# Reordering the first stages of an attention-plus-feed-forward kernel and splitting its last tile

## The chip, the cores and the metric

The kernel runs on one core of a Trainium2 chip. The core has five engines with instruction queues of their own, each worked off in order: TensorE (PE in the profile; its weight loads are listed as PEld), VectorE (DVE), ScalarE (ACT), GpSimd (POOL) and SyncE (SP). PE multiplies 128x128 blocks and writes to PSUM, a memory that the kernel divides into eight banks of 512 float32 values in each of 128 partitions; DVE and ACT read PSUM and write SBUF, the working memory. SP, ACT and POOL issue DMA transfers, which share 16 DMA engines.

The metric is device time in microseconds (us), the median of several executions. Beside it there is one profiled execution, whose span runs from its first to its last instruction.

## What is computed

Attention with a relative position bias over 8 batches and 8 heads of 576 positions, and then a bilinear feed-forward layer over the 4608 tokens:

```python
scores = scale * np.matmul(q, k.transpose(0, 1, 3, 2))      # q, k, v: 8 x 8 x 576 x 64
scores = scores + bias.transpose(2, 0, 1)[None, :, :, :]    # from a table of 32 buckets
scores = scores - np.max(scores, axis=-1, keepdims=True)
attn = np.exp(scores)
attn = attn / (np.sum(attn, axis=-1, keepdims=True) + 1e-09)
x = np.matmul(attn, v).transpose(0, 2, 1, 3).reshape(B * S, H * D)   # 4608 x 512
a = x @ w_a                                                 # 512 x 1536
b = x @ w_b
return (a * b @ w_out).astype(np.float32)                   # 1536 x 512
```

## The kernel before

**Units of work.** Heads are taken two at a time: 32 pairs, four to a batch. Of the 576 positions of a head, 512 are the main part (four tiles of 128) and 64 the tail; the tails of a pair's two heads share one tile. For pair `p`:

- `qk1(p, t)`: scores of key tile `t` against all main queries, one 512-column matmul per head, each on 64 rows of the array (in the profile the two start together). They go to one of two score buffers (`sc`, two banks each).
- `ex(p, t)`: ACT takes the exponential of both heads (128x1024) into an `at` tile, which frees the score buffer.
- `mul(p, t)`: DVE multiplies the part of `at` near the diagonal by the exponentials of the bias, `W`, which POOL and SP load from a small table in DRAM.
- `qk_tail`, `ex_tail`, `mul_tail`: the same for the tails (two exponentials on ACT).
- `av(p, j)`: query tile `j` of the product with v, with a column of ones that gives the sum; `norm(p, 0)` and `norm(p, 3)`: DVE's reciprocal and multiplication into `XG`, for tiles 0 to 2 and 3 to 4. Each frees an `av` bank.
- `t_x`, `c_x`: PE transposes `XG` and a copy puts it into `xn`, the feed-forward layer's input.
- `t_q`, `c_q`, `t_k`, `c_k` (pairs below 12): PE transposes q and k of a pair to come, and a copy puts them into `QT` and `KT`. For pairs 0, 1 and 3 this is done in float32 straight from `q32` and `k32` (`t32`, `q_next`, `k_next`; `tails_next` for the tails). From batch 3 on DMA does it.

The feed-forward layer is cut into nine chunks of 512 tokens. A chunk has 24 units, `ff_a` and `ff_b` for each of 12 blocks of 128 hidden columns (four matmuls; ACT copies `pa` to `ha`, DVE multiplies `pb` by `ha` into `g`), and 12 more, three parts for each of four output tiles (`ff_o`: four matmuls each; after the third ACT copies `po` to `ob` and SP stores it). The ninth chunk holds the tails of all heads, so each of its output tiles is stored in two DMAs (L536 to L538).

**Banks.** Two `sc` buffers (four banks), one bank `AV`, one `TR`, two of the pool `ffn` (`FF`). A bank of a pool is given to the next tile that asks for it once everything that reads it is done. From pair 12 on the feed-forward units also use `TR`.

**Order.** It is written out by hand (`manual_schedule`): each engine gets its instructions in the order in which the Python code makes them. First come the loads. SP and ACT issue those of pairs 0 and 1 in float32 (L184 to L187) and of the tails, POOL all others, one after another. PE starts with matmuls on a tile of zeros, `warm_up(5)` at L215 and L219, with the table's matmul between them. Then the transposes of pair 0 (L561 to L571), its first two score tiles (L572, L573), a loop over pairs 0 to 2 (L601 to L638), pair 3 and the start of pair 4 written out (L644 to L695), and from L714 a loop over pairs 4 to 32 that lays feed-forward units (`U`) between the steps of pair `s` and the `av` steps of pair `s - 1`. `quotas` says how many units a pair gets, and they are spread evenly over its `U` places. What is left of the units comes at L765.

Behind `k_next(0)` DVE sets one element of the tiles of pair 3 (L611, L612), and SP's loads of pair 3 (L613, L614) wait for that.

Of the kernel before, what the change touches and what calls it, by code (L numbers as in the profile page):

```python
# [13 lines left out]
def kernel(  # L14
# [11 lines left out]
    nc = tc.nc  # L26
    FP32 = mybir.dt.float32
# [9 lines left out]
    DM = 512  # L37
# [142 lines left out]
    def load32(p, src, out, engs):  # L180
        for h in range(2):
            load_h(engs[h], src, out[:, p, :, h, :], 0, 2 * p + h)
# [27 lines left out]
    def warm_up(n):  # L210
        for _ in range(n):
            nc.tensor.matmul(out=warm[:, :], lhsT=zero_sb[:, 0:128], rhs=zero_sb[:, :],
                             start=True, stop=True)
# [2 lines left out]
    tps = ps_av.tile([128, 512], FP32, tag="av", name="tab_ps")  # L216
    nc.tensor.matmul(out=tps[0:H, 0:NR], lhsT=bt_sb[0:NB, :], rhs=oh_sb[0:NB, :],
                     start=True, stop=True)
    warm_up(5)  # L219
    nc.scalar.activation(out=tab_sb[0:H, 127:127 + NR], in_=tps[0:H, 0:NR], func=ACTF.Exp)  # L220
    nc.scalar.dma_start(out=tab.ap(), in_=tab_sb[0:H, :])

# [108 lines left out]
        nc.sync.dma_start_transpose(  # L331
            out=dst[i][:, :, :, :].rearrange("d t h p -> d (t h) p"), in_=src[i][:, :])

    def qk1(p, t):
        qT = qT_(p)
        ps = ps_sc.tile([128, 2, 512], FP32, tag="sc", name=f"qk{p}_{t}")
        for hh in range(2):
            r = slice(64 * hh, 64 * hh + 64)
            nc.tensor.matmul(out=ps[:, hh, :], lhsT=kT_(p, t)[r, :],  # L339
                             rhs=qT[r, :, :], start=True, stop=True)  # L340
        st[p]["ps", t] = ps

    def qk(p, t0):
        qk1(p, t0)
        qk1(p, t0 + 1)

    def ex(p, t):
        ps = st[p]["ps", t]
        at = atp.tile([128, 2, SM], BF16, tag="at", name=f"at{p}_{t}")
        nc.scalar.activation(out=at[:, :, :], in_=ps[:, :, :], func=ACTF.Exp, scale=scale)  # L350
        st[p]["at", t] = at

    def mul(p, t):
        at, w = st[p]["at", t], W_sb[p % 4]
        lo, hi = max(0, 128 * (t - 1)), min(SM, 128 * (t + 2))
        y = 383 - (lo - 128 * (t - 1))
        z = y - (hi - lo)
        nc.vector.tensor_tensor(out=at[:, :, lo:hi], in0=at[:, :, lo:hi],  # L358
                                in1=w[:, :, y:(None if z < 0 else z):-1], op=MULT)
# [21 lines left out]
    def mul_tail(p):  # L381
        hp = p % 4
        at, w = att_sb[p % 2], W_sb[hp]
        nc.vector.tensor_tensor(out=at[:, 896:1088], in0=at[:, 896:1088],
                                in1=Wt_sb[:, hp, ::-1], op=MULT)
        x = at[:, 0:512].rearrange("p (h t c) -> p h t c", h=2, t=NM)[:, :, NM - 1, :]
        nc.vector.tensor_tensor(out=x, in0=x, in1=w[:, :, 127:63:-1], op=MULT)
# [86 lines left out]
    def c_x(p, eng=None):  # L474
        b, hp = divmod(p, 4)
        if p in XD:
            return
        ps = st[p]["x"]
        main, rest = xc(b)
        copy(eng, xn_sb[hp][:, main], ps[:, 0:SM])  # L480
        copy(eng, xn_sb[hp][:, rest], ps[:, SM:S])
# [36 lines left out]
    def ff_b(c, df, m0=0):  # L518
        ff_mm(c, df, wb_sb, "pb", m0, NMC)
        nc.vector.tensor_tensor(out=g_sb[df][:, :], in0=ff["pb"][:, :], in1=ff["ha"][:, :], op=MULT)  # L520

    def ff_o(c, tt, part):
        if part == 0:
            ff["po"] = ff_bank(f"po{c}_{tt}")
        po = ff["po"]
        for df in range(4 * part, 4 * part + 4):
            nc.tensor.matmul(out=po[:, :], lhsT=g_sb[df][:, 128 * tt:128 * tt + 128],  # L527
                             rhs=wo_sb[:, df, :], start=(df == 0), stop=(df == NDF - 1))
        if part == 2:
            ob = obp.tile([128, DM], FP32, tag="ob", name=f"ob{c}_{tt}")  # L530
            nc.scalar.activation(out=ob[:, :], in_=po[:, :], func=ACTF.Copy)  # L531
            if c < B:
                r0 = S * c + 128 * tt
                nc.sync.dma_start(out=out[r0:r0 + 128, :], in_=ob[:, :])
            else:
                for hh in range(2):  # L536
                    r0 = S * (2 * tt + hh) + SM
                    nc.sync.dma_start(out=out[r0:r0 + ST, :], in_=ob[64 * hh:64 * hh + 64, :])  # L538

    units = []  # L540
    for c in range(NCH):
        for df in range(NDF):
            m0 = 3 if c == 0 and df == 0 else 0
            units.append(lambda c=c, df=df, m0=m0: ff_a(c, df, m0))
            units.append(lambda c=c, df=df, m0=m0: ff_b(c, df, m0))
        for tt in range(4):
            for part in range(3):
                units.append(lambda c=c, tt=tt, part=part: ff_o(c, tt, part))
    nxt = 0

    def put_units(n):
# [18 lines left out]
    copy(None, QT[0][:, 256:512], psq1[:, 256:512])  # L570
    copy(None, KT[0][:, 128:SM], psk1[:, 128:512])  # L571
    qk1(0, 0)  # L572
    qk1(0, 1)  # L573

    def q_next(s):
        ps = bank(TR, BF16 if s == 1 else FP32, f"trq{s + 1}")
# [21 lines left out]
        for i in range(n):  # L598
            copy(eng, KT[(p0 + i) % 2][:, SM:SM + 256], ps[:, 256 * i:256 * i + 256])

    for s in range(3):  # L601
        ex(s, 0)
        if s > 0:
            mul(s - 1, 3)
            mul_tail(s - 1)
        q_next(s)
        qk1(s, 2)
        ex(s, 1)
        k_next(s)
        if s == 0:  # L610
            nc.vector.memset(q32[0:1, 3, 0, 0, 0:1], 0.0)  # L611
            nc.vector.memset(k32[0:1, 3, 0, 0, 0:1], 0.0)  # L612
            load32(3, q, q32, (nc.sync, nc.sync))  # L613
            load32(3, k, k32, (nc.sync, nc.sync))  # L614
        qk1(s, 3)
        ex(s, 2)
        if s == 0:
            tails_next(0, 2, None)
        else:
            tails_next(s + 1, 1, ACT)  # L620
        qk_tail(s)
        mul(s, 0)
        if s > 0:
            av(s - 1, 0)
            av(s - 1, 1)
            av(s - 1, 2)
            norm(s - 1, 0)
        mul(s, 1)
        ex(s, 3)
        if s > 0:  # L630
            av(s - 1, 3, FF)
        qk1(s + 1, 0)
        ex_tail(s)
        if s > 0:
            av(s - 1, 4)
            norm(s - 1, 3)
        mul(s, 2)
        qk1(s + 1, 1)  # L638

# [26 lines left out]
    t_x(2, FF)  # L666
    mul(3, 1)
    av_part(3, 0)
    c_x(2)
    t_q(4, FF)  # L670
    t_k(4, FF)
    c_q(4, ACT)
# [8 lines left out]
    qk1(4, 0)  # L681
    ex(4, 0)
    qk1(4, 1)
    ff_mm(0, 0, wa_sb, "pa", 0, 3)
    norm(3, 0)
    ex(4, 1)
    norm(3, 3)
    t_x(3, AV, range(3))
    ff_mm(0, 0, wb_sb, "pb", 0, 3)
    t_x(3, AV, range(3, 5))  # L690
    qk1(4, 2)
    ex(4, 2)
    c_x(3)
    qk1(4, 3)
    ex(4, 3)  # L695

    def tails4():
        ps = bank(TR, BF16, "trt4")
# [15 lines left out]
    for s in range(4, NP + 1):  # L714
        new = s < NP
        U = "unit"
        A = lambda *jq: (lambda: [av(s - 1, j, AV if j < 3 or s >= R3 else TR) for j in jq])
        N = lambda j: (lambda: norm(s - 1, j))
        steps = []
        if s == R3:  # L720
            ring3 = True
        if s == 4:
            steps += [U, tails4, lambda: mul(4, 0), U, lambda: qk_tail(4), lambda: ex_tail(4), lambda: mul(4, 1), U, lambda: mul(4, 2),
                      U, lambda: mul(4, 3), lambda: mul_tail(4), U, lambda: t_q(5, TR), lambda: c_q(5),
                      U, lambda: t_k(5, TR), lambda: c_k(5)]
        elif new:
            e = early((s + 1) // 4)
            steps += [lambda: qk(s, 0), lambda: ex(s, 0), U, lambda: ex(s, 1), A(0, 1, 2), N(0), U,
                      lambda: mul(s, 0), A(3, 4), N(3)]
            if s - 1 in XD:  # L730
                steps += [lambda: t_x(s - 1), lambda: turns(s)]
            steps += [U, lambda: mul(s, 1), lambda: qk(s, 2), lambda: ex(s, 2)]
            if e:
                steps += [lambda: t_q(s + 1, TR), lambda: c_q(s + 1)]
            steps += [U, lambda: ex(s, 3)]
            if e:
                steps += [lambda: t_k(s + 1, TR), lambda: c_k(s + 1)]
            steps += [U, lambda: mul(s, 2), U, lambda: mul(s, 3),
                      lambda: qk_tail(s), lambda: ex_tail(s), U]
            if s - 1 not in XD:  # L740
                steps += [lambda: t_x(s - 1, TR), lambda: c_x(s - 1), lambda: turns(s)]
            steps += [U, lambda: mul_tail(s), U]
        else:
            steps += [A(0, 1, 2), N(0), U, A(3, 4), N(3), U, lambda: t_x(s - 1, AV),
                      lambda: c_x(s - 1), U, U, U, U, U, U, U]
        quota = quotas.get(s, 9)
        seen, put = 0, 0
        nu = sum(1 for x in steps if x is U)
        for x in steps:
            if x is U:  # L750
                seen += 1
                n = (quota * seen + nu - 1) // nu - put
                put_units(n)
                put += n
            else:
                x()
        b = s // 4 + 1
        if new and s % 4 == 2 and b + 1 < B:
            load_qkt(b + 1)
        if new and 2 <= b < B:  # L760
            if s % 4 == 0:
                load_v(b)
                if b % 2 == 0:
                    load_vt(b, 2)
# [31 lines left out]
```

## Time and profile before

| What | us |
| --- | --- |
| Median of 5 runs | 427.04 (426.11 to 427.69) |
| The profiled execution | 426.11 |
| Its span, first to last instruction | 424.1 |

The profile's stretches, as busy time of each engine in us:

| Stretch (us) | what runs | PE | DVE | ACT | POOL | DMA GB/s |
| --- | --- | --- | --- | --- | --- | --- |
| 0 to 7.9 | loads, warm-ups, first transposes | 6.70 | 2.58 | 2.04 | 7.00 | 164 |
| 7.9 to 36.96 | pairs 0 to 3, first scores of pair 4 | 24.71 | 19.54 | 25.53 | 26.52 | 179 |
| 36.96 to 48.09 | rest of pair 4, first units | 10.14 | 7.03 | 4.02 | 9.02 | 168 |
| 48.09 to 122 | pairs 5 to 11 and units | 72.68 | 43.81 | 48.82 | 36.44 | 125 |
| 122 to 419.2 | the other pairs and units | 296.82 | 126.14 | 162.05 | 40.57 | 75 |
| 419.2 to 424.1 | last copy and store | 0.00 | 0.00 | 0.60 | 0.00 | 74 |

A line of the profile names an engine, the line of the kernel (L339 is the scores' matmul, L350 the exponentials, L508 the matmuls of `ff_a` and `ff_b`), the operation, the tiles as out<-in with their numbers left out (`qk`, `trq`, `trk`, `pa`), the shapes, and how often it came. In a list by time the first two numbers are the start and the length, and a bracket at the end is the idle time of the engine before it, with what ended it. Matmuls overlap: one of 512 columns lasts 0.38 us there, while a row of four lasts about 1.03 us.

### The profile page before, as it was taken

The page shows a single profiled execution, that of the slowest core. Times are in us where ns is not written, and L with a number is a line of the kernel's source. Part 1 is how long each engine was busy: PE and PEld are TensorE (multiplying, and loading weights), DVE is VectorE, ACT ScalarE, POOL GpSimd, SP SyncE. Part 2 cuts the span into 40 slices and gives each one's busy share as a digit, 9 for nine tenths or more (in the row PEclk, how much of TensorE's full clock was granted, in tenths as well). Part 3 has the DMA queues.
Part 4 walks back from the last instruction along what each step waited for, and adds up shares of the span by engine and source line. Part 5 has one row for each costly group of instructions (what it writes and reads, how often), then busy time and mean ns, then how long its engine had stood idle before and what let it go on. Part 6 is the DMA issues. An engine that isn't in the chain of part 4 may idle for free.

```text
span 424.1 us, 8476 instructions
## 1 busy us (share of the span) xinstructions
PE 411.1 (97%) x3410; PEld 204.0 (48%) x3410; DVE 199.1 (47%) x492; ACT 243.0 (57%) x343; POOL 119.5 (28%) x161
## 2 busy tenths in 40 slices
PE   8898999999999999999999999999999999999995
PEld 3573455555544444444444444444444454444442
DVE  3685576556552555245535553355425550431320
ACT  3986376666655666676656665666556642322321
POOL 9989829703528000920073003000000000000000
PEclk9999999999999999999999999999999999999999
DMA  9999999994929940999099908831021012002004
GB/s 163 184 174 166 164 171 141 177 181 37 102 24 179 167 60 15 129 190 123 15 95 197 137 15 57 170 74 31 15 88 33 8 17 99 2 0 100 0 4 96
DMA packets 162855, 40.31 MB, mean 95 GB/s; under 512 B 153368, under 2 KB 158016, under 8 KB 162816
## 3 DMA queue, kind: packets, MB, share of 16 engines
q0 software_dynamic: 110448, 18.75, 59.0%
q1 hardware_dynamic: 51248, 20.72, 24.9%
q8 instruction: 26, 0.43, 0.4%
q10 hardware_dynamic: 1120, 0.30, 0.3%
q14 instruction: 13, 0.11, 0.1%
HBM read 38.77 MB, written 9.45 MB: 114 GB/s over the span
## 4 chain that ended last, share of the span: by engine, by line
PE 91%; POOL 4%; DMA 3%; DVE 1%; ACT 0%; issue 0%; POOLq 0%; DVEq 0%
PE pa L508 23%; PE po L527 22%; PE pb L508 22%; PE av L409 8%; PE qk L339 7%; PE av L400 3%; DMA vm<-in_v_dram 2%; DMA qtl<-in_q_dram 1%; PE qkt L364 1%; PE qkt L367 1%; PE trx L472 1%; PE trq L291 1%; POOL kn L129 1%; POOL W L166 0%; PE trk L311 0%
## 5 line engine op out<-in xcount | busy, mean ns | idle before, releaser
L350 ACT ACTIVATE at<-qk 128x1024 bf16<-128x1024 f32 x128 | 126.0, 1023 | 21.9 <-PE qk L339 21.9
L520 DVE TENSOR_TENSOR g<-pb,ha 128x512 bf16<-128x512 f32 x108 | 74.7, 692 | 116.6 <-PE pb L508 96.6
L508 PE MATMUL pa<-xn,wa 128*128 128x512 bf16 x432 | 111.2, 379 | 1.6 <-ACT ha L515 1.6
L508 PE MATMUL pb<-xn,wb 128*128 128x512 bf16 x432 | 111.2, 379 | 0.0
L515 ACT ACTIVATE ha<-pa 128x512 f32<-128x512 f32 x108 | 64.6, 598 | 70.8 <-PE pa L508 69.3
L527 PE MATMUL po<-wo,g 128*128 128x512 bf16 x432 | 102.8, 379 | 0.0
L358 DVE TENSOR_TENSOR at<-at,W 128x512 bf16<-128x512 bf16 (+1 forms) x128 | 60.1, 483 | 9.7 <-ACT at L350 8.2
L508 PEld LDWEIGHTS <-wa 128*128 128x128 bf16 x432 | 38.9, 98 | 49.5 <-issue 10.3
L531 ACT ACTIVATE ob<-po 128x512 f32<-128x512 f32 x36 | 21.5, 598 | 69.9 <-PE po L527 69.9
L508 PEld LDWEIGHTS <-wb 128*128 128x128 bf16 x432 | 39.2, 98 | 45.5 <-issue 5.4
L527 PEld LDWEIGHTS <-g 128*128 128x128 bf16 x432 | 38.3, 98 | 45.5 <-issue 7.4
L123 POOL DMA_DIRECT2D vm<-in_v_dram x32 | 28.1, 904 | 103.0 <-PE av L409 102.2
L409 PE MATMUL av<-vm,at 128*128 128x65 bf16 x992 | 43.3, 193 | 0.0
L409 PEld LDWEIGHTS <-at 128*128 128x128 bf16 x992 | 39.5, 97 | 3.9
L445 DVE RECIPROCAL rc<-av 128x6 f32<-128x6 f32 x64 | 12.1, 188 | 57.3 <-PE av L409 55.5
L400 PE MATMUL av<-vt,att 128*128 128x130 bf16 x156 | 34.9, 224 | 0.4
L378 ACT ACTIVATE att<-qkt 128x1024 bf16<-128x1024 f32 x32 | 32.6, 1019 | 0.0
L446 DVE TENSOR_TENSOR XG<-av,rc 128x384 bf16<-128x384 f32 x64 | 31.4, 491 | 2.2
L123 POOL DMA_DIRECT2D qn<-in_q_dram x28 | 24.4, 915 | 26.8 <-PE trq L291 19.2
L123 POOL DMA_DIRECT2D kn<-in_k_dram x28 | 24.5, 910 | 4.2 <-DMA wb<-in_moe_w_b_dram 1.9
L339 PE MATMUL qk<-QTb,KTb 64*128 64x512 bf16 x160 | 24.2, 381 | 0.0
L400 PEld LDWEIGHTS <-att 128*128 128x128 bf16 x156 | 15.3, 98 | 15.3 <-DVE XG L446 10.7
(114 smaller groups left out, 240.9 us busy)
## 6 DMA issues: line engine op xcount, KB each, us to landing
out_dram<-ob SPq DMA_DIRECT2D x32, 256.0 KB, 3.5
vm<-in_v_dram POOLq DMA_DIRECT2D x28, 128.0 KB, 5.3
qn<-in_q_dram POOLq DMA_DIRECT2D x24, 128.0 KB, 8.5
kn<-in_k_dram POOLq DMA_DIRECT2D x24, 128.0 KB, 8.3
wa<-in_moe_w_a_dram POOLq DMA_DIRECT2D x3, 512.0 KB, 7.5
wb<-in_moe_w_b_dram POOLq DMA_DIRECT2D x3, 512.0 KB, 9.9
wo<-in_moe_w_out_dram POOLq DMA_DIRECT2D x1, 1536.0 KB, 13.5
out_dram<-ob SPq DMA_DIRECT2D x8, 128.0 KB, 2.4
```

The lines of the kernel that those rows point to most:

```text
L123: nc.gpsimd.dma_start(out=(vm[b % 2][:, h0:h1, t, 0:Dh] if dst is None else dst[b % 2][:, :].rearrange("p (t h d) -> p t h d", h=H, t=NM)[ ...
L339: nc.tensor.matmul(out=ps[:, hh, :], lhsT=kT_(p, t)[r, :], rhs=qT[r, :, :], start=True, stop=True)
L350: nc.scalar.activation(out=at[:, :, :], in_=ps[:, :, :], func=ACTF.Exp, scale=scale)
L358: nc.vector.tensor_tensor(out=at[:, :, lo:hi], in0=at[:, :, lo:hi], in1=w[:, :, y:(None if z < 0 else z):-1], op=MULT)
L378: nc.scalar.activation(out=at[:, 0:1024].rearrange("p (a x) -> p a x", a=2), in_=ps[:, :, :], func=ACTF.Exp, scale=scale)
L400: nc.tensor.matmul(out=pav[:, slot, :, :], lhsT=x, rhs=vt[b // 2 % 2][:, 4 * i + hp, :, 0:Dh + 1], start=fresh, stop=True, skip_group_chec ...
L409: nc.tensor.matmul(out=pav[:, slot, hh, :], lhsT=x, rhs=vm[i][:, 2 * hp + hh, t, 0:Dh + 1], start=False, stop=True, skip_group_check=True)
L446: nc.vector.tensor_tensor(out=xg[:, j0:j0 + n, :, :], in0=pav[:, 0:n, :, 0:Dh], in1=rc.unsqueeze(3).to_broadcast([128, n, 2, Dh]), op=MULT)
L508: nc.tensor.matmul(out=ff[key][:, :], lhsT=w[df // FW][:, mc, 128 * (df % FW):128 * (df % FW) + 128], rhs=xn_sb[mc][:, xin(c)], start=(i = ...
L515: nc.scalar.activation(out=ha[:, :], in_=ff["pa"][:, :], func=ACTF.Copy)
L520: nc.vector.tensor_tensor(out=g_sb[df][:, :], in0=ff["pb"][:, :], in1=ff["ha"][:, :], op=MULT)
L527: nc.tensor.matmul(out=po[:, :], lhsT=g_sb[df][:, 128 * tt:128 * tt + 128], rhs=wo_sb[:, df, :], start=(df == 0), stop=(df == NDF - 1))
```

## The change

Six places of the order are changed, and the number of real matmuls stays the same.

1. The second `warm_up(5)` becomes `warm_up(1)`. `qk1` gets an argument `fill`: so many 512-column matmuls on zeros into the score buffer ahead of the real ones. `qk1(0, 1)` and `qk1(0, 2)` get one each.
2. Pair 0 is written out in place of the loop's first round. `qk1(1, 0)` and `ex(1, 0)` now come ahead of `qk_tail(0)` and `ex_tail(0)`; `qk1(1, 1)` comes after `mul(0, 2)`. The loop runs over pairs 1 and 2.
3. `c_x(2)` goes from DVE to ACT.
4. The scores and exponentials of tiles 2 and 3 of pair 4 go from the stretch written out into pair 4's list of steps, behind the first three feed-forward units. In the stretch, `ex(4, 1)`, both `norm` and the first transposes of `XG` come ahead of `ff_mm` for `pa`, the other transposes ahead of `ff_mm` for `pb`. The list has 11 `U` places instead of 6 for the same 12 units, the last two of them behind `c_k(5)`.
5. In pairs 5 to 10, `t_q(s + 1)` and `c_q(s + 1)` come ahead of `qk(s, 2)` and `ex(s, 2)`.
6. The last output tile goes through `ff_last`: 12 matmuls of 256 columns, a copy on ACT, two stores (SP and ACT); then 12 for the other 256 columns, a copy on DVE, two stores.

```diff
@@ -216,7 +216,7 @@
-    warm_up(5)
+    warm_up(1)
     nc.scalar.activation(out=tab_sb[0:H, 127:127 + NR], in_=tps[0:H, 0:NR], func=ACTF.Exp)
@@ -331,9 +331,12 @@
-    def qk1(p, t):
+    def qk1(p, t, fill=0):
         qT = qT_(p)
         ps = ps_sc.tile([128, 2, 512], FP32, tag="sc", name=f"qk{p}_{t}")
+        for _ in range(fill):
+            nc.tensor.matmul(out=ps[:, 0, :], lhsT=zero_sb[:, 0:128], rhs=zero_sb[:, :],
+                             start=True, stop=True)
@@ -519,6 +522,18 @@
+    def ff_last(c, tt):
+        po = ff_bank(f"po{c}_{tt}")
+        ob = obp.tile([128, DM], FP32, tag="ob", name=f"ob{c}_{tt}")
+        for x, cols in enumerate((slice(0, 256), slice(256, 512))):
+            for df in range(NDF):
+                nc.tensor.matmul(out=po[:, cols], lhsT=g_sb[df][:, 128 * tt:128 * tt + 128],
+                                 rhs=wo_sb[:, df, cols], start=(df == 0), stop=(df == NDF - 1))
+            copy(None if x else nc.scalar, ob[:, cols], po[:, cols])
+            for hh, eng in enumerate((nc.sync, nc.scalar)):
+                r0 = S * (2 * tt + hh) + SM
+                eng.dma_start(out=out[r0:r0 + ST, cols], in_=ob[64 * hh:64 * hh + 64, cols])
+
@@ -570,7 +592,7 @@
     qk1(0, 0)
-    qk1(0, 1)
+    qk1(0, 1, 1)
@@ -598,42 +620,52 @@
-    for s in range(3):
-        ex(s, 0)
-        if s > 0:
-            mul(s - 1, 3)
-            mul_tail(s - 1)
+    ex(0, 0)
+    q_next(0)
+    qk1(0, 2, 1)
+    ex(0, 1)
+    k_next(0)
+    nc.vector.memset(q32[0:1, 3, 0, 0, 0:1], 0.0)
+    nc.vector.memset(k32[0:1, 3, 0, 0, 0:1], 0.0)
+    load32(3, q, q32, (nc.sync, nc.sync))
+    load32(3, k, k32, (nc.sync, nc.sync))
+    qk1(0, 3)
+    ex(0, 2)
+    tails_next(0, 2, None)
+    qk1(1, 0)
+    ex(0, 3)
+    ex(1, 0)
+    qk_tail(0)
+    mul(0, 0)
+    mul(0, 1)
+    ex_tail(0)
+    mul(0, 2)
+    qk1(1, 1)
+    for s in (1, 2):
+        if s > 1:
+            ex(s, 0)
+        mul(s - 1, 3)
+        mul_tail(s - 1)
...
@@ -666,7 +698,7 @@
-    c_x(2)
+    c_x(2, ACT)
@@ -681,18 +713,14 @@
     qk1(4, 0)
     ex(4, 0)
     qk1(4, 1)
-    ff_mm(0, 0, wa_sb, "pa", 0, 3)
+    ex(4, 1)
     norm(3, 0)
-    ex(4, 1)
     norm(3, 3)
     t_x(3, AV, range(3))
+    ff_mm(0, 0, wa_sb, "pa", 0, 3)
+    t_x(3, AV, range(3, 5))
     ff_mm(0, 0, wb_sb, "pb", 0, 3)
-    t_x(3, AV, range(3, 5))
-    qk1(4, 2)
-    ex(4, 2)
     c_x(3)
-    qk1(4, 3)
-    ex(4, 3)
@@ -720,19 +748,21 @@
-            steps += [U, tails4, lambda: mul(4, 0), U, lambda: qk_tail(4), lambda: ex_tail(4), lambda: mul(4, 1), U, lambda: mul(4, 2),
-                      U, lambda: mul(4, 3), lambda: mul_tail(4), U, lambda: t_q(5, TR), lambda: c_q(5),
-                      U, lambda: t_k(5, TR), lambda: c_k(5)]
+            steps += [U, U, lambda: qk1(4, 2), lambda: ex(4, 2), U, lambda: qk1(4, 3), lambda: ex(4, 3),
+                      lambda: mul(4, 0), U, tails4, U, lambda: qk_tail(4), lambda: ex_tail(4),
+                      lambda: mul(4, 1), U, lambda: mul(4, 2), U, lambda: mul(4, 3),
+                      lambda: mul_tail(4), U, lambda: t_q(5, TR), lambda: c_q(5), U,
+                      lambda: t_k(5, TR), lambda: c_k(5), U, U]
...
-            steps += [U, lambda: mul(s, 1), lambda: qk(s, 2), lambda: ex(s, 2)]
+            steps += [U, lambda: mul(s, 1)]
             if e:
                 steps += [lambda: t_q(s + 1, TR), lambda: c_q(s + 1)]
-            steps += [U, lambda: ex(s, 3)]
+            steps += [lambda: qk(s, 2), lambda: ex(s, 2), U, lambda: ex(s, 3)]
```

## The prediction

> **What bounds the kernel now.** First the page's busy times, then the list of waits of TensorE (who waited for whom: us in total, times, longest).
>
> ```profile
> PE 411.1 (97%) x3410; PEld 204.0 (48%) x3410; DVE 199.1 (47%) x492; ACT 243.0 (57%) x343; POOL 119.5 (28%) x161
> ```
>
> ```profile
> PE pa L508 <- ACT ha L515: 1.6, 1, 1.6
> ...
> PE qk L339 <- DVE KT L257: 1.2, 2, 1.0
> PE trk L311 <- DVE QT L257: 1.0, 2, 0.5
> PE qk L339 <- ACT att L378: 0.9, 1, 0.9
> ```
>
> TensorE (PE) is the bound: 97% busy, and all its listed waits come before 90 us. So an edit is worth what it moves on PE in the first 90 us, plus what lies behind the last matmul. The timeline shows the four stretches that count; columns are start, length, engine, line, operation, and in brackets the idle time before it.
>
> ```profile
> 6.50 0.42 PE L559 MATMUL trk0a<-id,k 128*128 128x128 f32 x1
> 8.72 3.77 ACT L350 ACTIVATE at<-qk 128x1024 bf16<-128x1024 f32 x4 [0.96 <-PE qk L339]
> 12.92 0.22 ACT L377 ACTIVATE att<-qktt 128x64 bf16<-128x64 f32 x1 [0.42 <-PE qktt L370]
> 13.94 1.70 DVE L358 TENSOR_TENSOR at<-at,W 128x512 bf16<-128x512 bf16 x4 [1.45 <-DMA W<-bias_tab]
> 16.86 0.38 PE L364 MATMUL qkt<-KT 128*128 128x128 bf16 x4 [0.16 <-ACT at L350]
> 29.59 0.51 DVE L257 COPY xn<-trx 128x512 bf16<-128x512 bf16 x2
> 30.25 0.38 PE L311 MATMUL trk<-cst_sb,kn 128*128 128x128 bf16 x4 [0.29 <-DMA qtl<-in_q_dram]
> ...
> 34.48 1.94 ACT L350 ACTIVATE at<-qk 128x1024 bf16<-128x1024 f32 x2 [0.28 <-PE qk L339]
> ...
> 36.30 0.60 ACT L515 ACTIVATE ha<-pa 128x512 f32<-128x512 f32 x1
> ...
> 36.96 1.02 PE L508 MATMUL pa<-xn,wa 128*128 128x512 bf16 x4 [1.63 <-ACT ha L515]
> ...
> 48.09 0.61 PE L339 MATMUL qk<-QT,KT 64*128 64x512 bf16 x4 [0.98 <-DVE KT L257]
> ...
> 62.14 0.60 PE L339 MATMUL qk<-QT,KT 64*128 64x512 bf16 x4
> 62.46 0.42 DVE L446 TENSOR_TENSOR XG<-av,rc 128x256 bf16<-128x256 f32 x1
> 62.94 0.40 PE L291 MATMUL trq<-cst_sb,qn 128*128 128x128 bf16 x4 [0.20 <-DVE XG L446]
> ...
> 419.23 0.60 ACT L531 ACTIVATE ob<-po 128x512 f32<-128x512 f32 x1 [1.99 <-PE po L527]
> 419.85 1.10 SPq L538 DMA_DIRECT2D out_dram<-ob  x2
> ```
>
> From 8.72 ScalarE (ACT) computes exponentials with one gap, 0.42, until about 16.8, where PE still waits for it; from 16.86 to 35 PE is dense. So what ACT gains before 16.86 is what PE gains at 16.86. The wait at 30.25 is named a DMA, but the copy `c_x(2)` at 29.59 ends at 30.10 and frees the bank that these transposes write: I take it as the releaser. At 36.96 PE waits for a bank that the copy at 36.30 frees, and that copy stands behind the two exponentials from 34.48. The page's clock row reads full from the start, yet f32 transposes last 421 ns before 7.6 us and 272 ns from 9.2 on: the early clock has to be read off durations.
>
> **The start.** Four warm-ups of 0.43 (five in 2.31) go. The first transpose then waits for pair 0's k: issued at 1.76, 3.7 to landing, 5.46. Weight load at 5.55 (6.08 before), matmul 0.23 later at 5.78 instead of 6.50: 0.72 earlier, not 1.7. The first scores follow at 7.57 instead of 8.29, but at the slow rate they last 0.63 (as a warm-up does) instead of 0.39, so the first exponential starts at 8.22: **-0.50**. PE idles from 4.9 to 5.55 meanwhile. The two fill matmuls cost 0.22 to 0.43 each; one sits in PE's wait for the K copy (0.20 at 8.88), one in its wait for the score bank that the first exponential frees.
>
> The clock can spoil this. With the slow rate until pair 0's fourth score, four f32 transposes take 0.85 instead of 0.45 and the fill and score 0.43 each: the third exponential is 0.67 late, 0.75 in all. With the fast rate from 7.5 on it costs nothing. The four k transposes from 7.57 took 0.66 in all, so the rate changed near 7.8 after 6.6 us of nearly unbroken matmuls, and the kernel keeps 6.6 less 1.7. I take nothing, since both sides of the comparison meet that change at an unknown moment, and keep 0.75.
>
> The Trainium skill, "TensorE: Matmul & The Clock Gate", Part 1, says that the array runs at half rate until a free-running window of 3.4 us was busy. The trace agrees in the halving (transposes start 0.213 apart before 7.6, about 0.11 apart after 9.2) but shows 6.6 us of matmuls ahead of the change. The rule speaks against the change, since a hole of 0.65 us is opened inside that window; by it the full rate could come one window later, near 11.3, and the sum would be 0.75 worse.
>
> **Pair 1's scores ahead of pair 0's tails.** ACT's 0.42 at 12.92 waits for the tails' scores, which wait for their key copies. Now a fifth exponential (0.94) runs there, and the tails' scores are ready by 12.6 when ACT asks at 12.9: **-0.42**. ACT's work until 16.81 is the same, so PE's `qk_tail(1)` starts at 15.9. Does something else hold it? W of pair 0 lands at 9.46 + 4.4 = 13.84, a load on POOL's queue that nothing here moves, so VectorE's (DVE's) multiplies start at 13.94 as before; they end with the tails' at 15.94, and `av(0,0)`, now at 16.4 instead of 17.35, finds them ready with 0.4 to spare. W of pair 1 lands at 16.23, before its use at 16.52. The k of pair 3 lands at 19.06, used at 20.61, now 19.7; W of pair 2 at 21.55, used at 22.49, now 21.55; wb at 31.2, used at 33.1 or later. All just fit. SP's four loads for pair 3 stay behind the two DVE memsets, which come 0.5 earlier; nothing waits behind them on SP.
>
> **`c_x(2)` on ACT.** ACT is busy with the last exponential until 29.66 (28.7 now) and needs 0.60 + 0.2 where DVE needed 0.51; `t_k(4)` gets its bank at 29.55 instead of 29.2: **+0.3** (0 to 0.6). Behind it on ACT stand `c_q(4)` and `c_k(4)`, 0.4 later, which `qk1(4,0)`, 1.58 after `t_k(4)` on PE, doesn't notice. DVE gains 0.5 that nobody waits for.
>
> **Pair 4.** In the old times: the two `qk1(4,2)`, `qk1(4,3)` leave PE's order at 34; `t_x(3)` now waits for XG, ready at 32.67 (0.35 lost, and all of PE behind it); `pa` 0.65, transposes, `pb` 0.65; `ff_a(0,0)` at 34.42; its ACT copy, no longer behind two exponentials, ends at 35.45; the next `pa`, which needs that bank, starts at 35.5 instead of 36.96. From there to pair 5's first scores PE has ten units of 0.864, the two moved scores (0.32 each), tails 0.13, `qk_tail` 0.5, `t_q` 0.22, `t_k` 0.33: 10.5, and I find one stall of 0.31 (`pa03`'s copy behind `ex_tail`) and 0.3 around `t_k(5)`. DVE's K copy at 48.09 is now covered by two units (1.73). Pair 5 starts at 35.5 + 11.1 = 46.6 instead of 48.09: **-1.49** (if both stalls double -0.9; without them -2.1).
>
> **Transposes ahead of scores, pairs 5 to 10.** `t_q` writes the bank that `norm`'s XG frees. Before, the 0.54 of scores stood between. At pair 6 PE would arrive at 62.14 and XG ends at 62.88: 0.80 of wait replaces 0.26, +0.54. Read in the same way, PE at the scores against the end of XG (behind `t_q` stand the scores, and behind them ACT's exponentials, which have 0.3 to 1.2 of idle time there): pair 5 52.83 and 53.11, +0.36; pair 9 89.09 and 88.97, 0; pair 10 100.99 and 101.27, +0.33. At pairs 7 and 8 PE also waited 0.52 each for the Q copy ahead of `t_k`; the scores now stand there, and although `t_q` starts 0.35 late `t_k` comes at 73.0 and 81.2 instead of 73.17 and 81.42: -0.37. Sum **+0.86**. Ends: -1.24 if XG is always ready, and +4.9 for DVE one g (0.69) later at each.
>
> **The last tile.** Twelve matmuls of 256 columns take 1.3; the tile starts at 416.43. No row of before shows PE writing one part of a bank while another engine reads the rest; every bank is written again only after its reader's end. So I let the second half wait: first half drained 417.9, ACT's copy (0.38 for 256 columns) 418.35, second half drained 419.85, DVE's copy (0.42) 420.3, two issues side by side on SP and ACT, landing 2.3 later at 422.6. Now: 419.85, second issue 420.37, landing 422.73. **-0.2**; without the wait 0.65 earlier, -0.75. Four issues instead of two, with nothing behind them. The Trainium skill, "PSUM — Partial Sum Buffer", section on bank collisions, asks for a guard by bank rather than by address; no run here shows a case; by it the sum has -0.2, without it -0.75.
>
> **Sum.** -0.50 - 0.42 + 0.30 - 1.49 + 0.86 - 0.20 = -1.45. Against its own execution (426.11, span 424.1 and 2.0 around it): 424.66. That execution is the lowest of five, 0.93 under the median; the change is a difference, so from 427.04: **425.6**.
>
> **Rivals.** *The clock comes later*: +0.75, 426.3. For it the removed matmuls; against it the fills, and that the first transposes keep PE busy. *Loads hold the start*: -0.92 is lost at W or at pair 3's k, 426.5. For it the 1.45 at 13.94; against it the margins above. *Every cover holds*: turns -1.24 instead of +0.86, 423.5, and 422.9 with the tail's halves free. *Slower*: DVE runs one g later ahead of `t_q` in pairs 5 to 10, so PE waits 6.2 there in all, a term of +4.9 instead of +0.86: 429.6. For it: at pair 5 a g already stands ahead of XG; against it pair 9. It decides once DVE is 0.25 later in each than now.
>
> **Chances.** Forecast 0.44 (0.31 faster, 0.13 within), covers 0.12 (faster), clock 0.16 (0.05, 0.10, 0.01 slower), loads 0.10 (0.03, 0.06, 0.01), slower rival 0.18 (0.03 within, 0.15). Faster by over 0.3% (1.28 us, about what a measurement of this kernel can tell from no change) 0.51, within 0.32, slower 0.17. The forecast's own range is 424.0 to 426.9; with the covers and part of the slower rival 423.2 to 427.9.
>
> **What would show it.** Right: first transposes near 5.8, first exponential near 8.2, no ACT gap before pair 0's tails, `qk_tail(1)` near 15.9, the second `pa` near 34.9, no wait at pair 5's first scores, waits for XG ahead of `trq` in pairs 5, 6 and 10. Wrong: f32 transposes still at 421 ns after 9 us; `t_k(4)` as late as 30.2; more than 3.8 of XG waits; second-half matmuls with no gap.

## Result and profile after

| | before | after |
| --- | --- | --- |
| Median (runs) | 426.91 (66), range 425.66 to 429.39 | 425.58 (38), range 425.04 to 427.01 |
| The profiled execution | 426.11 | 425.21 |
| Its span | 424.1 | 423.4 |

The ratio of the times is 0.9971, with a 95% interval from 0.9963 to 0.9978. The forecast was 425.6. The total came out as forecast; the terms of the sum did not all do so, and a part of the gain came by a way that was not in it.

First the list of TensorE's waits after the change (us in total, times, longest):

```profile
PE trq L291 <- DVE XG L449: 2.4, 5, 0.7
...
PE trk0a L581 <- DMA k<-in_k_dram: 0.7, 1, 0.7
PE po L530 <- ACT ob L255: 0.5, 1, 0.5
PE pa L511 <- ACT ha L518: 0.5, 1, 0.5
...
PE trk L311 <- ACT xn L255: 0.4, 1, 0.4
```

The wait of `pa` for `ha` fell from 1.6 to 0.5, the waits for the K and Q copies ahead of `qk` and `trk` are gone, and waits of `trq` for `XG` (2.4, against 0.2) have taken their place. The last tile has a wait in the middle that was not there. Next the places that the prediction named, in a list by time (start, length, engine, line, operation; the bracket is the idle time before it):

```profile
5.69 0.45 PE L581 MATMUL trk0a<-id,k 128*128 128x128 f32 x1 [0.68 <-DMA k<-in_k_dram]
...
8.21 1.02 ACT L353 ACTIVATE at<-qk 128x1024 bf16<-128x1024 f32 x1 [1.23 <-PE qk L342]
...
12.40 0.40 PE L367 MATMUL qkt<-KT 128*128 128x128 bf16 x4 [0.20 <-DVE KT L257]
...
16.18 0.38 PE L367 MATMUL qkt<-KT 128*128 128x128 bf16 x4 [0.16 <-ACT at L353]
...
29.84 0.38 PE L311 MATMUL trk<-cst_sb,kn 128*128 128x128 bf16 x4 [0.36 <-ACT xn L255]
...
34.98 1.02 PE L511 MATMUL pa<-xn,wa 128*128 128x512 bf16 x4 [0.47 <-ACT ha L518]
...
45.88 0.60 PE L342 MATMUL qk<-QT,KT 64*128 64x512 bf16 x4
...
61.26 0.40 PE L291 MATMUL trq<-cst_sb,qn 128*128 128x128 bf16 x4 [0.74 <-DVE XG L449]
...
100.42 0.40 PE L291 MATMUL trq<-cst_sb,qn 128*128 128x128 bf16 x4 [0.64 <-DVE XG L449]
...
415.97 1.47 PE L530 MATMUL po<-wo,g 128*128 128x256 bf16 x12
...
417.91 1.47 PE L530 MATMUL po<-wo,g 128*128 128x256 bf16 x12 [0.47 <-ACT ob L255]
```

And pair 0's tails in the kernel before:

```profile
12.21 0.40 PE L364 MATMUL qkt<-KT 128*128 128x128 bf16 x4 [0.52 <-DVE KT L257]
```

Read against before: the first transposes come at 5.69 instead of 6.50 and the first exponential at 8.21 instead of 8.72, yet pair 0's tails (12.40) come later than before (12.21). Pair 1's tails, 16.18, are 0.68 ahead. Pair 4's first scores are 0.41 ahead (31.42 against 31.83), the second `pa` 1.98, pair 5's first scores 2.21. By the last tile only 0.46 of that is left (415.97 against 416.43): pairs 5 to 10 give back 1.75. Behind it 0.19 is won. So the two profiled executions add up to -0.41 - 1.80 + 1.75 - 0.19 = -0.65, the difference of the spans.

The medians differ by 1.33, not by 0.65. The runs themselves say why: each lists its mean granted clock. Of 98 runs of the kernel before that were made beside the experiments, 40 have a clock of 0.998 or more and a median of 426.18, and 58 have 0.985 to 0.996 and a median of 427.59. All 39 listed runs of the changed kernel (the 38 and the profiled one) have 0.998 or more; in the profiled one the missing 0.002 lies behind the last matmul, from 421.73 to the end at 423.4, where the clock is at half and PE has nothing to do. At full clock the change is therefore worth 425.58 - 426.18 = -0.60, as in the traces; the rest is that the lower clock doesn't occur. What this lower clock is came out of the fourth experiment.

### The profile page after: what moved, and what is told of

It reads as the page before. It is cut to its first block, busy times and chain, and to the rows that moved or that the text cites. A ratio compares the mean times of both kernels' runs of the same rounds, so it can differ in the third digit from the quotient of the medians.

```text
span 423.4 us, 8500 instructions
## 1 busy us (share of the span) xinstructions
PE 411.7 (97%) x3420; PEld 204.6 (48%) x3420; DVE 199.4 (47%) x491; ACT 243.9 (58%) x345; POOL 119.5 (28%) x161
## 4 chain that ended last, share of the span: by engine, by line
PE 93%; DVE 2%; DMA 2%; ACT 2%; issue 1%; SPq 0%; ACTq 0%; DVEq 0%
PE pb L511 22%; PE pa L511 22%; PE po L542 21%; PE av L412 8%; PE qk L342 8%; PE av L403 3%; PE qkt L367 2%; PE qkt L370 2%; DMA kt<-in_k_dram 1%; DVE XG L449 1%; DMA k<-in_k_dram 1%; PE trx L475 1%; ACT at L353 1%; PE po L530 1%; PE trq L291 1%
## 5 line engine op out<-in xcount | busy, mean ns | idle before, releaser
L542 PE MATMUL po<-wo,g 128*128 128x512 bf16 x420 | 100.2, 379 | 0.0
L542 PEld LDWEIGHTS <-g 128*128 128x128 bf16 x420 | 37.2, 98 | 44.0 <-issue 7.4
L403 PE MATMUL av<-vt,att 128*128 128x130 bf16 x156 | 34.9, 224 | 0.4
```

The lines of the kernel that those rows point to most:

```text
L403: nc.tensor.matmul(out=pav[:, slot, :, :], lhsT=x, rhs=vt[b // 2 % 2][:, 4 * i + hp, :, 0:Dh + 1], start=fresh, stop=True, skip_group_chec ...
```

## The experiments

Each kernel below was run twelve times, the first two and the last six times, beside runs of the kernel before on the same chip. "Against the change" means the difference of the medians to 425.58, "the turn" part 5 (in pairs 5 to 10 `t_q` ahead of the scores). The ratio is to the kernel before, with its 95% interval in brackets; these reach 0.6 to 0.9 us to either side, so differences of a few tenths between medians are weak evidence, and the traces are read beside them.

**1. Scores first again in pairs 5 to 10.** Part 5 is undone.

```diff
-            if e:
-                steps += [lambda: t_q(s + 1, TR), lambda: c_q(s + 1)]
-            steps += [lambda: qk(s, 2), lambda: ex(s, 2), U, lambda: ex(s, 3)]
+            steps += [lambda: qk(s, 2), lambda: ex(s, 2)]
+            if e:
+                steps += [lambda: t_q(s + 1, TR), lambda: c_q(s + 1)]
+            steps += [U, lambda: ex(s, 3)]
```

> The changed kernel with part 5 undone: in pairs 5 to 10 the scores of tiles 2 and 3 stand ahead of t_q again. Theory (the order itself costs what the starts of the pairs show, +1.75 from pair 5 to pair 11): 425.58 - 1.75 = 423.8, and the two waits of 0.5 ahead of t_k in pairs 7 and 8 come back inside it. Rival (DVE is late there in any order, so the wait only moves behind the scores): less than half of that comes back, 424.7 or more.

Measured: 424.25 (423.71 to 424.85), ratio 0.9936 [0.9917, 0.9954], 1.33 better than the change. In its list of waits the ones for `XG` ahead of `trq` are gone, and the two for the Q copy are back:

```profile
PE trk L311 <- DVE QT L257: 1.0, 2, 0.5
```

From pair 4's tails to the last matmul it takes 378.43 where the change takes 379.98, -1.55. So part 5 costs 1.3 to 1.6, nearly the 1.75 read from the trace of the change; the theory's 423.8 is closer than the rival's 424.7.

**2. The new turn in pairs 7 and 8 alone**, where the trace shows a gain.

```diff
+            first = s in (7, 8)
+            if not first:
+                steps += [lambda: qk(s, 2), lambda: ex(s, 2)]
             if e:
                 steps += [lambda: t_q(s + 1, TR), lambda: c_q(s + 1)]
-            steps += [lambda: qk(s, 2), lambda: ex(s, 2), U, lambda: ex(s, 3)]
+            if first:
+                steps += [lambda: qk(s, 2), lambda: ex(s, 2)]
+            steps += [U, lambda: ex(s, 3)]
```

> t_q ahead of the scores in pairs 7 and 8 alone, where the feed-forward units leave no unit between c_q and t_k. Theory: as the run with all scores first, less the 0.26 that pairs 7 and 8 gained together: 423.5. Rival: that 0.26 is noise of one trace, and the time is the same as with all scores first.

Measured: 424.36 (423.27 to 424.85), the same as without any new turn. In the traces the two pairs, from pair 7's first scores to pair 9's, take 16.25 where experiment 1 and the kernel before take 16.51. The gain of 0.26 is the one expected, and the medians of six runs can't show it; the prediction had 0.37.

**3. Pair 4 as before.** Part 4 is undone: scores and exponentials of tiles 2 and 3 back in the stretch, six `U` places.

```diff
-    ex(4, 1)
+    ff_mm(0, 0, wa_sb, "pa", 0, 3)
     norm(3, 0)
+    ex(4, 1)
     norm(3, 3)
     t_x(3, AV, range(3))
-    ff_mm(0, 0, wa_sb, "pa", 0, 3)
+    ff_mm(0, 0, wb_sb, "pb", 0, 3)
     t_x(3, AV, range(3, 5))
-    ff_mm(0, 0, wb_sb, "pb", 0, 3)
+    qk1(4, 2)
+    ex(4, 2)
     c_x(3)
+    qk1(4, 3)
+    ex(4, 3)
...
```

> The changed kernel with part 4 undone (pair 4 as before). Theory: the wait of 1.6 for ha and the one of 1.0 for the K copy return, +1.80 as the starts of pair 5 show: 427.4. Rival: pair 4's order was only a place where PE caught up with loads or DVE, and waits later shrink in turn: +1.0 or less, 426.6.

Measured: 427.40 (426.94 to 428.61), ratio 1.0013 [0.9997, 1.0028], 1.82 against the change. The two waits that part 4 was seen to remove are back:

```profile
PE pa L511 <- ACT ha L518: 1.6, 1, 1.6
...
PE qk L342 <- DVE KT L257: 1.0, 1, 1.0
```

**4. The old start.** Parts 1 and 2 are undone: ten warm-ups, no fills, pair 0 in the old order.

```diff
-    warm_up(1)
+    warm_up(5)
...
-    qk1(0, 1, 1)
+    qk1(0, 1)
...
-    ex(0, 0)
...
-    qk1(1, 1)
-    for s in (1, 2):
-        if s > 1:
-            ex(s, 0)
+    for s in range(3):
+        ex(s, 0)
...
```

> The changed kernel with the start of before (two times five warm-ups, no fills, pair 0 in the loop's order). Theory (the start is worth what the two profiles differ by at pair 4's first scores, 0.41): 426.0, with a spread like that of the changed kernel (most runs within 0.5 of its median). Rival (the start also makes the spread of before, whose median lies 0.8 above its profiled run against 0.4 here): 426.6 or more, with runs from 425.6 to over 427.5.

Measured: 425.89 (425.44 to 428.52), ratio 0.9981 [0.9964, 0.9998]. The median is where the theory put it and the spread where the rival put it: seven runs at full clock have a median of 425.67, five have 0.986 to 0.996 and go up to 428.52. The profiled one is the 428.52. Its stretches (busy time of PE, PEld, DVE, ACT and POOL, then the granted clock, the DMA share and GB/s), cut where its clock changes (4.88, 11.70 and 21.94) and between these in equal parts, and a few lines of its list by time:

```profile
4.88:8.29 3.41, 3.15 (x21) 1.77 (x19) 1.18 (x3) 1.31 (x3) 3.41 (x6) 1.00 1.80 194
8.29:11.70 3.41, 1.63 (x11) 0.97 (x11) 1.39 (x4) 2.85 (x4) 3.41 (x6) 1.00 2.45 159
11.70:15.10 3.40, 2.35 (x13) 1.10 (x12) 1.38 (x4) 1.03 (x3) 3.40 (x5) 0.50 1.20 191
15.10:18.50 3.40, 3.24 (x17) 1.48 (x17) 2.40 (x8) 2.92 (x4) 2.63 (x5) 0.50 1.91 216
18.50:21.94 3.44, 3.22 (x45) 2.97 (x44) 0.84 (x3) 2.33 (x4) 2.87 (x4) 0.50 1.75 153
```

```profile
9.35 0.39 PE L342 MATMUL qk<-QT,KT 64*128 64x512 bf16 x2
11.46 0.30 PE L618 MATMUL trt<-id,kt 128*128 128x128 f32 x1 [1.72 <-DMA kt<-in_k_dram]
...
13.96 0.61 PE L342 MATMUL qk<-QT,KT 64*128 64x512 bf16 x2
```

PE ran out of work and waited 1.72 for the tails' keys. In the stretch of 3.41 around it PE was busy for 1.63, 48%. From the end of that stretch the clock is at half for three further stretches of the same length, though PE is busy for 69%, 95% and 94% of them; the same scores last 0.61 instead of 0.39. This also reads the other runs: 3.41 at half clock is 1.7 of 424, or 0.004 of the mean clock, and the lower clocks of the kernel before lie in groups near 0.996, 0.992 and 0.989, as one, two and three such stretches would. That each of those runs holds such a stretch is inferred, since only this one has a profile. So the question of the next five runs was what in the start keeps the clock up.

**5. No fills** (`qk1(0, 1)` and `qk1(0, 2)` without them, the rest as changed).

```diff
-    qk1(0, 1, 1)
+    qk1(0, 1)
...
-    qk1(0, 2, 1)
+    qk1(0, 2)
```

> The changed kernel without its two fill matmuls. Theory (the clock: a stretch with little matmul work lets the slow rate stay longer or come back, and the fills keep PE busy there): median 426.2 or more, with runs above 427.5. Rival (the fills are idle work): 425.6, or 0.2 less, with no wider spread.

Measured: 425.84 (425.13 to 426.75), ratio 0.9967 [0.9951, 0.9983], no run under 0.998. The fills aren't what keeps the clock up.

**6. Ten warm-ups again**, with fills and the new order.

```diff
-    warm_up(1)
+    warm_up(5)
```

> The changed kernel with all ten warm-ups, its fills and its order kept. Theory (with ten warm-ups the fast rate can come near 5 us, PE then runs ahead into the wait for the tails' loads near 11.4, and the slow rate comes back, as in the profiled run with the old start): median 426, with runs up to 428 like those with the old start. Rival (the fills and pair 1's scores keep PE busy enough whatever the warm-ups): 425.6, no run over 427.

Measured: 425.65 (425.27 to 426.51), ratio 0.9961 [0.9944, 0.9977], 0.07 against the change and no run under 0.998. Fewer warm-ups are worth nothing by themselves. In its profile the first exponential comes at 8.01 and pair 0's tails at 12.45, with the change at 8.21 and 12.40. The list of waits says why:

```profile
PE trt L618 <- DMA kt<-in_k_dram: 0.6, 1, 0.6
```

The load of the tails' keys lands at 10.8 to 11.3 in every profile. Pair 0's tails need it, so whatever the start gains ahead of it PE waits for there.

**7. Old order, no fills, but the changed kernel's warm-ups** (five and then one, six in all). On the kernel of experiment 4:

```diff
-    warm_up(5)
+    warm_up(1)
```

> Part 2's order of pair 0 undone and no fills, but with the one warm-up of the changed kernel: what does the order of pair 0 do by itself? Theory: in the old order PE has nothing to do while it waits for the tails' keys (1.7 us with ten warm-ups in the run that went back to half rate, more here, since PE arrives earlier and the load still lands near 11.2), so several of the twelve runs go back to half rate: at least 3 with a granted clock of 0.996 or less, the runs spread over 2 us or more, median near 425.9. Rival: only the number of warm-ups, and so the moment at which the full rate opens, decides; with one warm-up no run is under 0.998, all lie within 1.6 us, and the median is that of the changed kernel, 425.3 to 425.8.

Measured: 425.68 (425.33 to 426.99), ratio 0.9974 [0.9961, 0.9988]. Three of twelve runs are at 0.996 or less, as the theory's bound had it, but the spread of 1.66 and the median lie nearer the rival. In the old order the clock falls with six warm-ups too; three runs of twelve against five in experiment 4 don't tell whether less often.

**8. New order, ten warm-ups, no fills.**

```diff
-    warm_up(1)
+    warm_up(5)
...
-    qk1(0, 1, 1)
+    qk1(0, 1)
...
-    qk1(0, 2, 1)
+    qk1(0, 2)
```

> Ten warm-ups and no fills as before the change, with only the order of pair 0 new. Theory: the order puts pair 1's scores and the fifth exponential where PE waited for the tails' keys, and that is what prevents the fall back to half rate: no run under 0.998, median 425.6 (425.3 to 425.9) with a spread under 1.6 us. Rival: warm-ups and fills prevent it; at least 3 of twelve runs at 0.996 or less, with a spread of 2 us or more.

Measured: 425.29 (424.87 to 426.49), ratio 0.9959 [0.9945, 0.9973], no run under 0.998. With the new order alone the clock stays up, and the start is at least as good as the changed one (by the medians 0.3 better, no more than such medians tell).

**9. The new order alone, in the kernel before.** The opposite way round: nothing else of the change.

```diff
-    for s in range(3):
-        ex(s, 0)
...
+    ex(0, 0)
+    q_next(0)
+    qk1(0, 2)
...
+    qk1(1, 0)
+    ex(0, 3)
+    ex(1, 0)
+    qk_tail(0)
...
+    qk1(1, 1)
+    for s in (1, 2):
...
```

> The kernel before with one part of the change alone: pair 0's new order (ten warm-ups, no fills, everything else as before). Of the 81 runs of the kernel before on these chips about three in five have a granted clock of 0.996 or less and lie near 427.7, the others near 426.2. Theory: the order alone keeps the full rate, so no run (one at most) is at 0.996 or less; the median is that of the runs of before at full rate, less the few tenths that the traces give the order: 425.9 (425.6 to 426.3), ratio near 0.997. Rival: the fall back to half rate hangs on something else of the changed kernel; five or more of twelve runs at 0.996 or less, the median within 0.3 of the kernel before's on the same chip (426.9 or more).

Measured: 425.91 (425.17 to 426.67), ratio 0.9977 [0.9963, 0.9992]; nine of twelve runs at 0.998 or more, two at 0.997, one at 0.993. Beside it 11 of 17 runs of the kernel before were at 0.996 or less, with a median of 427.01 over all 17. The order alone brings 1.1 of the median's gain, and most of it by the clock: of the runs at 0.998 or more the medians are 425.82 and 426.03. The traces fit: these are the stretches of 3.41 in which PE was least busy from 6 to 20, found by sliding such a stretch along PE's matmuls; first the kernel before, then the changed one:

```profile
11.65:15.06 3.41, 1.79 (x18) 1.04 (x17) 1.88 (x5) 2.98 (x5) 3.41 (x5) 1.00 1.14 189
```

```profile
11.90:15.31 3.41, 2.46 (x23) 1.40 (x22) 1.68 (x5) 3.32 (x6) 3.41 (x5) 1.00 1.15 192
```

PE is busy for 1.79 (53%) before and 2.46 (72%) after, since ACT's fifth exponential, and the scores that follow it on PE, now fill the hole. Found in the same way, the weakest stretch of experiment 4's profile (9.48 to 12.89) is busy for 1.17, 34%. The 48% above belong to the stretch that ends where the clock falls; the stretch that begins at the same distance from a change of the clock in the kernel before (11.32 to 14.74) has 2.00, 58%, and there the clock held. Where the limit lies these runs don't show, and the share in one profile doesn't rank the starts: the weakest stretches of experiments 8 and 9 have 53% and 52% (in 9 since W landed only at 15.2), and the clock held.

What stands is the count: with the new order 2 of 141 runs have 0.996 or less, with the old one 66 of 122. Three pairs of kernels differ in the order alone: experiments 4 and 8 (5 of 12 runs against 0 of 12), 7 and 5 (3 of 12 against 0 of 12), the kernel before and experiment 9 (58 of 98 against 1 of 12). Pair 4's old wait ahead of 36.96, which the change removes too, is as weak a stretch (33.55 to 36.96: 1.78, 52%), but it isn't what makes the clock fall by itself: experiments 3 and 9 have it with the new order, and 1 of their 24 runs is at 0.996 or less. That it is the hole in PE's work through which the order acts fits these counts and experiment 4's profile; with one profile of a fall it is argued, not shown.

Open is why the old order falls less often in experiments 4 and 7 (8 of 24) than in the kernel before. The gains of the order alone, 1.1, and of all but the start, about 1.2 (425.89 against 427.11 over the 98), add up to more than the whole gain of 1.5 over the 98. Most of this is the median's doing: it jumps when the runs at the lower clock become fewer than half. By the means the two gains are 0.9 (426.02 against 426.92) and 0.8 (426.30 against 427.11), and the whole 1.4 (425.71 against 427.11).

**10. Last tile's halves in two banks.** `ff_last` asks for a bank per half.

```diff
-        po = ff_bank(f"po{c}_{tt}")
...
         for x, cols in enumerate((slice(0, 256), slice(256, 512))):
+            po = ff_bank(f"po{c}_{tt}_{x}")
```

> The last tile's halves in two banks, so that the second half's matmuls need not wait for the copy of the first. Theory (the second half waits 0.47 and drains 0.17 for one bank): 425.58 - 0.65 = 424.9, no wait of PE at the last tile. Rival (the stores of the first half are in the way of those of the second, and the end doesn't move): 425.5.

Measured: 425.30 (424.44 to 425.87), ratio 0.9956 [0.9939, 0.9972], 0.28 better than the change by the medians. Its list by time:

```profile
417.25 2.78 PE L530 MATMUL po<-wo,g 128*128 128x256 bf16 x24
...
420.07 0.42 DVE L257 COPY ob<-po 128x256 f32<-128x256 f32 x1 [9.63 <-PE po L530]
```

The 24 matmuls run through in 2.78 where the change needs 3.41 (415.97 to 419.38). From the same mark (pair 13's tails) to the end it takes 284.38 against 285.08, -0.70, which is the size that the theory had; the medians, with 425.30 between the theory's 424.9 and the rival's 425.5, show less of it.

**11. Last tile whole.** Part 6 is undone.

```diff
-                if c == NCH - 1 and tt == 3:
+                if False:
```

> The last tile whole, as before, all else of the change kept. Theory (the halves give 0.2: 0.65 lost on PE, 0.84 won behind it): 425.8. Rival (splitting the copy and the stores is worth its whole 0.75): 426.3.

Measured: 426.16 (425.45 to 428.09), ratio 0.9981 [0.9963, 0.9998], 0.58 against the change. On the stretch from pair 13's tails to the end the trace has 285.29 against 285.08, 0.21 against it, as predicted. The medians would have it at nearly three times that; with runs that spread over 2.6 these are not told apart.

**12. What the runs speak for, put together.** The edits of experiments 2 and 10 together, and `c_x(2)` on DVE again; the start as changed.

```diff
-    c_x(2, ACT)
+    c_x(2)
```

> The changed kernel with t_q ahead of the scores in pairs 7 and 8 alone, the last tile's halves in two banks, and c_x(2) on DVE again. If the gains add: 425.6 less 1.3 (turns) less 0.28 (two banks) less 0.08 (c_x) = 423.9, ratio to the kernel before near 0.993. Rival: what the turns and c_x give back is work that PE then waits for elsewhere; 424.3 or more, no better than the turns alone.

Measured: 423.41 (422.87 to 423.89), ratio 0.9913 [0.9894, 0.9931]; all six runs lie below every run of both kernels. Against the change that is -2.17. The gains add: 1.33 for the turns (medians of experiment 1), 0.70 for the banks and 0.07 for `c_x(2)` (traces) make 2.10. The rival has a point in the profiled run all the same: PE waits 0.66 at 72.15 for a load of k (`kn`), a wait that the profiles of the change and of experiment 2 don't have, and pair 7 takes 9.13 there instead of 8.16.

## Why the prediction was right, and where it was not

| Term | Predicted | Traces | Undone alone, medians |
| --- | --- | --- | --- |
| Start: warm-ups and pair 0's order | -0.92 | -0.48 | -0.31 |
| `c_x(2)` on ACT | +0.30 | +0.07 | not run alone |
| Pair 4 | -1.49 | -1.80 | -1.82 |
| Turns, pairs 5 to 10 | +0.86 | +1.75 | +1.33 |
| Last tile | -0.20 | -0.19 | -0.58 |
| Sum | -1.45 | -0.65 | -1.38 |

**The total** was right because two errors cancel, and that is luck. In the traces the sum is 0.80 short of the forecast, mostly by the turns. What made up for it is the clock that doesn't fall back: the prediction looked at the clock for its first rise alone, and took nothing for it, "since both sides of the comparison meet that change at an unknown moment". By the medians the start looks small (-0.31) because only five of experiment 4's twelve runs have the lower clock; by the means it is -0.58.

**The start.** The first exponential came at 8.21 (8.22 predicted), but its 0.50 is worth nothing (experiment 6). The step that failed is "ACT's work until 16.81 is the same, so PE's `qk_tail(1)` starts at 15.9"; it starts at 16.18. The prediction followed W and pair 3's k, and left out the tails' own keys, which land near 11.1. In ten of the fourteen profiles pair 0's tails start at 12.1 to 12.6, whenever the first exponential came (7.43 to 8.72). In the change's own profile most of the 0.50 is gone even before that load: from 7.56 until then PE works with no listed wait, the two fills take 0.54 and 0.32 of that time, and pair 0's third scores come at 9.79, as before (9.80).

A further 0.2 of the lead goes behind pair 1's tails (0.68 there, 0.47 at pair 2's), and that is W, of which the prediction said that nothing here moves it. It landed at 14.3 instead of 13.8:

```profile
14.39 1.70 DVE L361 TENSOR_TENSOR at<-at,W 128x512 bf16<-128x512 bf16 x4 [1.71 <-ACT att L381]
```

The profile names ACT, but in all fourteen profiles this multiplication starts 0.10 behind the landing of W (13.8 to 15.2). Behind it on DVE stands the copy of the next pair's q, and `qktt` of pair 1 needs the bank that this copy frees. Where W is latest, in experiment 9, this is PE's second longest wait:

```profile
PE qktt L370 <- DVE QT L257: 1.3, 1, 1.3
```

There pair 1's tails are 0.88 ahead of before and pair 2's 0.39 behind. So the rival "loads hold the start" happened, at W and at a load that it didn't name. The order's -0.42 was right as a mechanism: the fifth exponential runs at 12.24 instead of 13.95. It was undersized, because with the old order the clock also falls in about half of the runs, and the sum had no term for that.

**The clock.** The rival "the clock comes later" was half right. With ten warm-ups the full clock begins at 4.9 to 7.9 (five profiles), with six at 8.7 to 12.1 in eight profiles and at 4.9 in a ninth; in that of the change at 8.72, 0.81 after that of before. Mostly the load hides this. In the three where it began at 10.8 to 12.1 (experiments 1, 5 and 10) it did not: pair 0's tails came at 13.1, 13.2 and 13.8, later than in the change's by 0.73, 0.76 and 1.44. Its bound of 0.75 was of the right size for two of them. (The "four k transposes from 7.57" of its reading are three; the moment that it took from them, 7.8, is near the 7.91 at which the profile's clock goes to full.)

**`c_x(2)` on ACT.** The named releaser was right: the wait ahead of `t_k(4)` is now put down to ACT's copy into `xn`. The lead over before falls from 0.48 at pair 3's tails to 0.41 at pair 4's first scores, 0.07 instead of 0.30.

**Pair 4.** Second `pa` 34.98 (34.9 predicted), pair 5's first scores with no wait. The lead there is 1.80 more than at 31.42; the prediction set 0.61 aside for stalls behind the second `pa`, and only 0.26 came (0.16 ahead of a `pa` at 41.78, 0.10 at 45.88), which is most of the surplus over 1.49.

**Turns.** The waits are at the pairs that were named, and pairs 7 and 8 gain, but the term was mis-sized: +0.52, +0.64, -0.26 (7 and 8 together), +0.04 and +0.81 where +0.36, +0.54, -0.37, 0 and +0.33 were predicted. More than half of the miss is pair 10. There PE is through with its `pa` and could start the transposes at 99.62, 2.33 behind the last `pb` (97.29); `XG` ends 3.07 behind it, while in the kernel before it ended 2.71 behind it. Two lines of DVE's list by time, first of the changed kernel, then of the one before:

```profile
98.79 0.69 DVE L523 TENSOR_TENSOR g<-pb,ha 128x512 bf16<-128x512 f32 x1 [0.51 <-PE pb L511]
...
99.94 0.42 DVE L449 TENSOR_TENSOR XG<-av,rc 128x256 bf16<-128x256 f32 x1
```

```profile
99.70 0.69 DVE L520 TENSOR_TENSOR g<-pb,ha 128x512 bf16<-128x512 f32 x1
...
100.85 0.42 DVE L446 TENSOR_TENSOR XG<-av,rc 128x256 bf16<-128x256 f32 x1
```

From `g` to the end of `XG` both take 1.57. But `g` starts 1.50 behind its first `pb` matmul after the change and 1.14 before it (98.56 to 99.70), and DVE was idle for 0.51. The prediction read DVE's ends as fixed against PE's and priced the order of PE alone.

The other profiles take the two apart. In experiments 4 and 7, which have the turn, this `g` starts after 1.14 as before, and pair 10 is 0.45 longer than before: that is the turn. In experiments 1 and 2, which don't have the turn in pair 10, `g` starts after 1.5, and the pair is 0.17 and 0.15 longer. So 0.36 of the 0.81 came with the late `g`. Why `g` is late is not shown. A trail is that in all nine profiles with the late `g` the trace lists 191 instructions of DVE ahead of it, and a packet of the DMA queue that the profile calls "q14 instruction" starts 0.66 to 0.92 behind its start; in the five others it is 192 to 194 instructions, and that packet starts 1.9 to 2.2 ahead of `g`. The delay may thus belong to a place in DVE's stream of instructions, where its next ones are loaded; no run tests this.

The slower rival (a whole `g` late in each pair) didn't happen.

**Last tile.** The second half does wait, 0.47, for ACT's copy of the first; halves free of this wait are worth 0.70 (experiment 10; 0.55 lay between the prediction's two ends).

## What to carry to other kernels

Follow every load that the first stages need, not only the ones that wait now: what is won ahead of a load that doesn't come earlier is waited for there. An order in which a bank's reader had time to finish behind other work is worth keeping; a step moved to where it shortens one wait is to be priced pair by pair at the engine that frees its bank. And where runs of one kernel spread by some tenths of a per cent, look at each run's granted clock before the trace: in experiment 4's profile a hole of 1.72 in TensorE's work was followed by 10.24 at half the clock.

## What the runs showed of the hardware

In experiment 4's profile, after one stretch of 3.41 in which PE was busy for 48%, with no hole longer than 1.72, the granted clock fell to half and stayed there for 10.24, three such stretches, two of which were busy for 94% and more. The Trainium skill, "TensorE: Matmul & The Clock Gate", in its section on why this matters for kernels, advises against idle gaps of more than about 3 us between bursts of matmuls; the trace shows the clock fall after a shorter one, so the measurement decides here. The moment at which the full clock begins also differs by more than two such stretches between kernels that are the same up to there: 4.88 in experiment 12 and 12.14 in experiment 10, both with six warm-ups.
